# All three tiles of p transposed by DMA in batches 1 to 3, in an attention kernel that feeds two dense layers

## The chip, the cores and the metric

The kernel runs on one core of a Trainium2 chip. The metric is the time of one execution in microseconds, the median over the runs of one kernel. TensorE (PE in the profile), VectorE (DVE), ScalarE (ACT), GpSimd (POOL) and SyncE (SP, which here issues every DMA of the kernel) each work through their own list of instructions in order and wait for one another through semaphores.

## What is computed

```python
# q, k, v: (4 batches, 8 heads, 1152 rows, 64), float32
q_pool = q.reshape(B, H, S // 2, 2, D).mean(axis=3)          # 576 queries per head
scores = (1.0 / np.sqrt(D)) * np.matmul(q_pool, k.transpose(0, 1, 3, 2))
attn = np.exp(scores - np.max(scores, axis=-1, keepdims=True))
attn = attn / (np.sum(attn, axis=-1, keepdims=True) + 1e-09)
x = heads side by side of np.matmul(attn, v)                 # 2304 x 512
h = x @ w_in                                                 # 512 -> 2048
x = np.where(h >= 1, h, np.where(h <= -1, 0.0, (h + 1) ** 2 / 4)) @ w_out    # 2048 -> 512
out = np.maximum(np.maximum(x @ w1, x @ w2), x @ w3) @ w_out2                # 512 -> 768 -> 512
```

## The kernel before

Attention is cut into 48 **units**: batch (4), block of 192 queries (3 per batch), pair of heads (4). A unit's 2 x 192 queries fill three tiles of 128 rows: tile 0 has the even head's first 128 queries, tile 1 the odd head's first 128, tile 2 the remaining 64 of each head. For each tile, `soft` forms the scores against all 1152 keys on PE (three PSUM banks), DVE takes the row maximum, ACT the exponential into `pf`, with the row sums beside it. The product with v needs the tile transposed, keys on partitions, and `turned` does that. In batch 0 (`WHOLE`) all is float32 and PE transposes. In batches 1 to 3, 36 units, numbers go to PE as two float16 halves, "hi" (rounded) and "lo" (the rest):

- tiles 0 and 1: ACT writes hi and DVE writes lo into `hl`, and one DMA transpose, issued by SP, moves both halves into `pt`;
- tile 2: PE transposes the float32 tile in nine 128 x 128 pieces into PSUM (`tr`), ACT writes hi and DVE lo from there into `pt`.

`shares` adds the 1e-9 to the three row sums (POOL), takes reciprocals (DVE), spreads them (POOL), has PE turn them into one row per head, `rs`, and copies that to `R` (ACT). `av` multiplies `pt` with v on PE, and DVE multiplies the result by `R` and a scale into `xf`.

The first dense layer follows for each block of 192 queries: eight **up steps** (`up_step`, 24 products on PE each) and four **down steps** (`down_step`, 48 products each). They are the filler that stands between the attention units on every engine. The last four down steps are written out a second time by the generator `dense` behind the two tables (this stays so). The second dense layer comes last; its weights w1 to w3 are loaded and split by the steps `h` and `j`, its input by `Z`, all in the table `AFTER`.

The order on each engine is written out by hand: the tables `ATTENTION` and `AFTER` name one step after another (`s13.2` is a step of unit 13's tile 2, `r` of `shares`, `a` of `av`, `u` and `y` of an up or down step, `k`, `v`, `q` of loading and splitting), and each name records the next piece of that step's generator on whichever engines it uses. Nothing is reordered behind them.

`pf` has 2 buffers, `hl` 3 (the tile of k before its own DMA transpose takes one of these too), `pt` 2. Scores and `tr` share two places of three PSUM banks each. POOL also pools q and splits k, v and q; SP also issues the loads of q, k, v and weights, the transposes and copies of q and k, and the stores of the first layer's result y.

Of the kernel before, what the change touches and what calls it, by code (L numbers as in the profile page):

```python
# [7 lines left out]
F32 = mybir.dt.float32  # L8
F16 = mybir.dt.float16
# [3 lines left out]
ALU = mybir.AluOpType  # L13
# [135 lines left out]
def body(ctx: ExitStack, tc: tile.TileContext, q, k, v, w_in, w_out, w1, w2, w3, w_o2, out):  # L149
# [283 lines left out]
    def q_steps(b, i, p):  # L433
# [58 lines left out]
    def soft(b, i, p, who):  # L492
# [4 lines left out]
        if who == 0:  # L497
            sums[b, i, p] = small.tile([P, 3], F32, tag="sm", bufs=4, name=f"sm{b}_{i}_{p}")
# [683 lines left out]
```

## Time and profile before

| | |
|---|---|
| median of three runs | 1137.13 us (1136.02 to 1138.56) |
| the profiled execution | 1133.35 us |
| its span, first to last instruction | 1131.6 us |
| busy share of the span: PE, weight loads of PE, DVE, ACT, POOL | 93%, 77%, 77%, 68%, 20% |
| chain of work that ended last: PE, DVE, ACT, DMA | 53%, 3%, 2%, 2% of the span |
| granted TensorE clock over the execution | 0.988 |

Busy shares are means over stages of different kinds. Batch 0 of attention and the preparation of weights fill roughly the first 230 us, batches 1 to 3 with the first dense layer between them run to about 770 us, the rest of the first dense layer to 857 us, and the second dense layer to the end. A stage's own row tells which engine has no time left in it. A DMA share of 1.00 would be all 16 DMA engines busy; since packets overlap, single rows go above it.

### The profile page before, as it was taken

Reading aid. Unit: us, or ns where it says so; the run is one execution under the profiler, and the core shown is the slowest. Engines: PE = TensorE matmul, PEld = TensorE weight load, DVE = VectorE, ACT = ScalarE, POOL = GpSimd, SP = SyncE. Lnnn points to the kernel's source line nnn. Section 1 sums busy time; section 2 is a strip of 40 time slices with the busy share of each in tenths; the row PEclk is TensorE's granted clock in tenths of the full one; section 3 lists DMA queues with packets and bytes.
Section 4 is the critical chain, followed back from the end, with each engine's and each line's share of the span. In section 5 each row is a group of like instructions: output and inputs, shape, how many; then the busy total and the mean of one; then the engine's idle time right before and its main releaser. Section 6 shows DMA issues by size and latency. Waiting matters only on the chain.

```text
span 1131.6 us, 27049 instructions
## 1 busy us (share of the span) xinstructions
PE 1053.1 (93%) x11175; PEld 875.4 (77%) x11175; DVE 866.8 (77%) x1422; ACT 768.9 (68%) x1354; POOL 226.4 (20%) x305
## 2 busy tenths in 40 slices
PE   1578998899999989999999999999999999999998
PEld 1355875678888878888888888899998877767774
DVE  6998896788888889887998887877875868364441
ACT  6697797778788778887888887775774443353332
POOL 3333223422212242121223211100000106000000
PEclk9898998999999999999999999999999999999999
DMA  9964324478578887766897766455444100100001
GB/s 330 256 169 162 103 73 95 126 161 148 91 138 155 171 170 155 138 134 110 169 183 150 137 114 105 94 86 189 155 121 137 43 10 20 61 11 19 20 19 56
DMA packets 274443, 135.31 MB, mean 120 GB/s; under 512 B 229136, under 2 KB 257552, under 8 KB 273296
## 3 DMA queue, kind: packets, MB, share of 16 engines
q1 hardware_dynamic: 274320, 133.59, 52.2%
q8 instruction: 87, 1.43, 0.5%
q14 instruction: 36, 0.29, 0.1%
HBM read 62.39 MB, written 9.83 MB: 64 GB/s over the span
## 4 chain that ended last, share of the span: by engine, by line
PE 53%; DVE 3%; ACT 2%; DMA 2%; issue 1%; POOL 1%; POOLq 0%; ACTq 0%; DVEq 0%; SPq 0%
PE py L691 11%; PE p L922 9%; PE ph L663 8%; PE po L1085 6%; PE sc L488 4%; PE pa L1020 4%; PE av L596 4%; PE pb L1020 2%; PE tr L551 2%; DVE st L502 1%; PE pc L1020 1%; DMA pt<-hl 1%; ACT pf L509 1%; DMA vn<-in_v_dram 1%; DVE hl L575 0%
## 5 line engine op out<-in xcount | busy, mean ns | idle before, releaser
L502 DVE TENSOR_REDUCE st<-sc 128x1 f32<-128x1152 f32 x144 | 194.4, 1352 | 34.2 <-PE sc L488 33.8
L691 PE MATMUL py<-g,wou 128*128 128x192 f16 x2496 | 213.3, 246 | 1.8 <-ACT t L667 1.6
L691 PEld LDWEIGHTS <-wou 128*128 128x128 f16 x2496 | 207.2, 98 | 2.4 <-issue 2.0
L663 PE MATMUL ph<-xh,win 128*128 128x192 f16 x2304 | 205.3, 247 | 0.2
L663 PEld LDWEIGHTS <-win 128*128 128x128 f16 x2304 | 191.5, 99 | 8.6 <-issue 4.3
L509 ACT ACTIVATE pf<-sc,st,esc 128x1152 f32<-128x1152 f32 x144 | 188.6, 1310 | 13.7 <-DVE st L504 9.5
L488 PE MATMUL sc<-kst,qst 128*64 128x512 f16 (+3 forms) x1152 | 168.8, 333 | 20.8 <-DMA kst<-kpre 7.0
L488 PEld LDWEIGHTS <-qst 128*64 128x64 f16 (+1 forms) x1152 | 79.9, 106 | 83.6 <-issue 30.8
L922 PE MATMUL p<-yh,wm 128*128 128x288 f16 x864 | 107.1, 286 | 0.0
L551 PE MATMUL tr<-ident,pf 128*128 128x128 f32 x648 | 87.0, 284 | 19.2 <-ACT pf L509 19.0
L922 PEld LDWEIGHTS <-wm 128*128 128x128 f16 x864 | 84.5, 98 | 21.9
L575 DVE TENSOR_TENSOR hl<-pf,hl 128x1152 f16<-128x1152 f32 x72 | 98.4, 1366 | 3.8 <-ACT hl L573 3.7
L551 PEld LDWEIGHTS tr<-ident,pf 128*128 128x128 f32 x648 | 74.3, 147 | 26.2 <-ACT pf L509 19.4
L596 PE MATMUL av<-pt,vhl 128*64 128x192 f16 x1944 | 86.8, 247 | 1.6 <-DMA pt<-hl 1.6
L596 PEld LDWEIGHTS <-vhl 128*64 128x64 f16 x1944 | 79.7, 110 | 6.9 <-issue 3.3
L573 ACT ACTIVATE hl<-pf 128x1152 f16<-128x1152 f32 x72 | 83.6, 1161 | 1.3
L667 ACT ACTIVATE t<-ph,Uv 128x384 f32<-128x384 f32 x96 | 55.0, 574 | 35.5 <-PE ph L663 31.1
L1085 PE MATMUL po<-wo,h 128*128 128x512 f16 (+1 forms) x342 | 72.3, 368 | 0.0
L519 POOL TENSOR_SCALAR sm<-sm 128x3 f32<-128x3 f32 x48 | 21.2, 442 | 248.4 <-ACT pf L509 239.9
L675 ACT ACTIVATE g<-t,dgs 128x384 f16<-128x384 f32 x96 | 57.7, 609 | 6.4 <-DVE t L673 5.6
L561 DVE TENSOR_TENSOR pt<-tr,pt 128x1152 f16<-128x1152 f32 x36 | 48.7, 1354 | 16.6 <-ACT pt L559 16.3
L677 DVE SCALAR_TENSOR_TENSOR g<-t,dgs,g 128x384 f16<-128x384 f32 x96 | 59.7, 632 | 2.1 <-ACT g L675 1.8
(211 smaller groups left out, 1565.4 us busy)
## 6 DMA issues: line engine op xcount, KB each, us to landing
vn<-in_v_dram SPq DMA_DIRECT2D x16, 576.0 KB, 4.7
kn<-in_k_dram SPq DMA_DIRECT2D x16, 576.0 KB, 4.8
raw_m<-in_moe_w_dram SPq DMA_DIRECT2D x12, 768.0 KB, 4.7
raw_in<-in_moe_w_in_dram SPq DMA_DIRECT2D x8, 1024.0 KB, 7.0
qn<-in_q_dram SPq DMA_DIRECT2D x24, 256.0 KB, 3.1
raw_ou<-in_moe_w_out_dram SPq DMA_DIRECT2D x10, 512.0 KB, 4.4
y_d<-ys SPq DMA_DIRECT2D x52, 96.0 KB, 2.1
qst<-qst SPq DMA_DIRECT2D x48, 96.0 KB, 2.3
```

What stands on the lines that cost most here:

```text
L488: nc.tensor.matmul(sc[m0:m1, n0:n1], qst[b, i, p][who][:, var, m0:m1], ks[:, h, n0:n1], start=(var == 0), stop=(var == 1))
L502: nc.vector.tensor_reduce(out=m, in_=sc, axis=AX.X, op=ALU.max, negate=True)
L509: nc.scalar.activation(out=pf, in_=sc, func=AF.Exp, bias=nb, scale=e, accum_out=sums[b, i, p][:, who:who + 1])
L551: nc.tensor.transpose(tr[:, c * P:(c + 1) * P], pf[:, c * P:(c + 1) * P], ident)
L573: nc.scalar.activation(out=hl[:, 0], in_=pf, func=AF.Copy)
L575: nc.vector.tensor_tensor(out=hl[:, 1], in0=pf, in1=hl[:, 0], op=ALU.subtract)
L596: nc.tensor.matmul(acc[64 * h:64 * h + 64], vhl[b, p][:, vi, h, c, :], pt[:, h, pi * KT + c, :], start=(c == 0 and e == 0), stop=(c == KT ...
L663: nc.tensor.matmul(ph[:, a], win[:, wi, kt, ff * P:(ff + 1) * P], x[:, xi, kt], start=(kt == 0 and e == 0), stop=(kt == KD - 1 and e == 2))
L691: nc.tensor.matmul(py, wou[:, ff // 2, wi, ff % 2, m * P:(m + 1) * P], g[:, gi, ff, :], start=(ff == 0 and e == 0), stop=(ff == NF - 1 and ...
L922: nc.tensor.matmul(ph[:, :NB2], wm[:, wi, i, kt, ff * P:(ff + 1) * P], yh[:, yi, kt, n0:n0 + NB2], start=(kt == 0 and e == 0), stop=(kt == ...
L1020: nc.tensor.matmul(ps[:, :NB2], w(wi, kt), x[:, xi, kt], start=(first and kt == 0 and e == 0), stop=(kt == 1 and e == 2), skip_group_check ...
L1085: nc.tensor.matmul(po, hh[:, hi, ff, t * P:(t + 1) * P], wo[:, wi, ff, c0:c1], start=(n == 0 and e == 0), stop=(n == NF2 - 1 and e == 2))
```

## The change

In batches 1 to 3, `turned` now does the same for all three tiles: POOL adds to the tile's own column of row sums and DVE takes its reciprocal; ACT writes hi and DVE lo from `pf`, both multiplied by that share; one DMA transpose moves both into `pt`. PE no longer transposes these tiles, `shares` is not called there, and `xf` needs only the scale, so ACT reads the product out of PSUM. `pt` is laid out as one row of 384 columns: tile 0, tile 2, tile 1. For that the odd head's queries are taken in another order, its first 64 rows into tile 2 and the following 128 into tile 1, so a q load that was one DMA for four head parts is now two. The small tiles `esc`, `sm` and `rb` have more buffers. In batch 0 only the spreading of tile 2's reciprocals is done in another way. Both tables are written anew.

```diff
-OWN_BANK = (True, False)
+BY_DMA = lambda b, i, p: True
+FOLD = False
 ATTENTION = """
-s42.0 s42.2 u8.6 u8.5 s42.1 u8.6 a41 s42.2 s42.1 s43.0 a41 s42.2 s42.1 u8.7 u8.6 s43.0 r42 s42.1 s42.2 u8.7 r42
+s41.2 s42.0 u8.7 s41.2 s41.1 s42.1 s41.2 s42.0 u8.6 s42.2 u8.5 s42.0 u8.6 y7.3 s41.2 s42.0 s42.2 s41.2 s42.1
...
     def q_steps(b, i, p):
-        load_q.dma_start(out=qn[:, 0:4].rearrange("p a r d -> p a (r d)"),
-                         in_=q[b, h0:h0 + 4, r0:r1].rearrange("h (p r) d -> p h (r d)", r=2))
+        shift = 0 if WHOLE(b, p) else P
+        for h in range(2 if shift else 1):
+            hs, r = (slice(h0 + h, h0 + 4, 2), r0 + h * shift) if shift else (slice(h0, h0 + 4), r0)
+            load_q.dma_start(out=qn[:, h:4:2 if shift else 1].rearrange("p a r d -> p a (r d)"),
+                             in_=q[b, hs, r:r + 2 * P].rearrange("h (p r) d -> p h (r d)", r=2))
...
     def turned(b, i, p, who, pf):
-            if not WHOLE(b, p):
-                tr = tr.rearrange("p (c h q) -> p h c q", c=KT, h=2)
-                hi, lo = pt[:, :, 0:KT, P:NB], pt[:, :, KT:2 * KT, P:NB]
-                nc.scalar.activation(out=hi, in_=tr, func=AF.Copy)
-                nc.vector.tensor_tensor(out=lo, in0=tr, in1=hi, op=ALU.subtract)
...
+        share = sums[b, i, p][:, who:who + 1]
+        at_ = slice(*((0, P), (2 * P, 3 * P), (P, 2 * P))[who])
+        nc.gpsimd.tensor_scalar(out=share, in0=share, scalar1=1e-9 * 2.0 ** 12, scalar2=2.0 ** -15, op0=ALU.add,
+                                op1=ALU.mult)
+        nc.vector.reciprocal(out=share, in_=share)
...
         hl = hlp.tile([P, 2, KT * P], F16, tag="hl", name=f"hl{key}")
-        nc.scalar.activation(out=hl[:, 0], in_=pf, func=AF.Copy)
-        nc.vector.tensor_tensor(out=hl[:, 1], in0=pf, in1=hl[:, 0], op=ALU.subtract)
-        nc.sync.dma_start_transpose(out=pt[:, who, :, 0:P], in_=hl.rearrange("p a b -> p (a b)"))
+        nc.scalar.activation(out=hl[:, 0], in_=pf, func=AF.Copy, scale=share)
+        nc.vector.scalar_tensor_tensor(out=hl[:, 1], in0=pf, scalar=share, in1=hl[:, 0], op0=ALU.mult, op1=ALU.subtract)
+        nc.sync.dma_start_transpose(out=new_pt(b, i, p)[:, :, at_], in_=hl.rearrange("p a b -> p (a b)"))
...
     def av(b, i, p):
-        nc.vector.scalar_tensor_tensor(out=xf[b, i][:, p, :], in0=acc, scalar=Uv[b][:, p:p + 1], in1=R.pop((b, i, p)),
-                                       op0=ALU.mult, op1=ALU.mult)
+            nc.scalar.activation(out=xf[b, i][:, p, :], in_=acc, func=AF.Copy, scale=Uv[b][:, p:p + 1])
```

How the tables move instructions is seen in the recorded order of each engine. First PE in batch 3, block 1, around tile 2 of pair 1 (names end in block, pair, tile and a buffer number; `tr` is the transposed tile, `py` and `ph` are down and up steps). Before:

```order
L551 MATMUL tr_1_1_2_10194<-ident,pf_1_1_2_10147 128x128 x9
L691 LDWEIGHTS wou
L691 MATMUL py_1_2_10207<-g_1_8505,wou 128x192
...
L488 LDWEIGHTS qst_1_2_9630
L488 MATMUL sc_1_2_1_10270<-kst_2_8727,qst_1_2_9630 128x512
...
L528 MATMUL tr_1_1_2_10194<-ident,rb_1_1_10191 128x128
L529 MATMUL tr_1_1_2_10194<-rb_1_1_10191,halves 128x64
L663 LDWEIGHTS win
L663 MATMUL ph_2_6_10285<-xh_2_8936,win 128x192
```

The changed kernel at the same place, from tile 2 of pair 1 to the product with v of pair 0:

```order
L498 MATMUL sc_1_1_2_9848<-kst_1_7971,qst_1_0_8775 64x512
...
L498 LDWEIGHTS qst_1_2_9367
L498 MATMUL sc_1_2_0_9865<-kst_2_8538,qst_1_2_9367 128x512
...
L696 LDWEIGHTS win
L696 MATMUL ph_2_6_9882<-xh_2_8778,win 128x192
...
L630 LDWEIGHTS vhl_0_7914
L630 MATMUL av_1_0_9916<-pt_1_0_9626,vhl_0_7914 64x192
```

The nine transposes of tile 2 and the two instructions that turn the sums are gone from PE, and the product with v of pair 0 now stands behind the scores of pair 1's last tile and pair 2's first. Over the whole of PE's list, 14 up steps and 15 down steps stood behind the last product with v; now 12 and 14 do, so two up steps and one down step have moved ahead of it.

DVE at the same place (`st` is the row maximum, `hl` lo of a tile, `sm` a reciprocal, `g` a piece of an up step). Before:

```order
L610 SCALAR_TENSOR_TENSOR xf_1_10104<-av_1_0_10028,Uv_9055,R_1_0_10083 128x192
L677 SCALAR_TENSOR_TENSOR g_2_9500<-t_2_2_3_9949,dgs_6817,g_2_9500 128x384
L502 TENSOR_REDUCE st_1_1_2_10118<-sc_1_1_2_10091 128x1
L575 TENSOR_TENSOR hl_1_1_1_10108<-pf_1_1_1_10089,hl_1_1_1_10108 128x1152
L502 TENSOR_REDUCE st_1_2_0_10177<-sc_1_2_0_10111 128x1
...
L561 TENSOR_TENSOR pt_1_1_10106<-tr_1_1_2_10194,pt_1_1_10106 128x2x9x64
```

And now, for the three tiles of pair 1:

```order
L581 RECIPROCAL sm_1_1_9722<-sm_1_1_9722 128x1
L512 TENSOR_REDUCE st_1_1_2_9875<-sc_1_1_2_9848 128x1
L600 SCALAR_TENSOR_TENSOR hl_1_1_0_9861<-pf_1_1_0_9783,sm_1_1_9722,hl_1_1_0_9861 128x1152
L512 TENSOR_REDUCE st_1_2_0_9912<-sc_1_2_0_9865 128x1
L600 SCALAR_TENSOR_TENSOR hl_1_1_1_9908<-pf_1_1_1_9844,sm_1_1_9722,hl_1_1_1_9908 128x1152
...
L581 RECIPROCAL sm_1_1_9722<-sm_1_1_9722 128x1
L512 TENSOR_REDUCE st_1_2_1_10025<-sc_1_2_1_9979 128x1
...
L581 RECIPROCAL sm_1_2_9911<-sm_1_2_9911 128x1
L600 SCALAR_TENSOR_TENSOR hl_1_1_2_10027<-pf_1_1_2_9972,sm_1_1_9722,hl_1_1_2_10027 128x1152
```

Lo of tile 2 is formed from `pf` like the others, one reciprocal stands ahead of each lo, and the multiplication into `xf` is no longer here.

SP in batch 2, block 1, pairs 1 and 2 (`pt` from `hl` is the transpose of a tile, `qst` and `qn` belong to q, `y_d` is a store of y). Before:

```order
L578 DMA_TRANSPOSE pt_1_1_6903<-hl_1_1_0_6826 128x18x128
L460 DMA_TRANSPOSE qst_2_0_6952<-qpre_2_0_6342 128x6x128
L578 DMA_TRANSPOSE pt_1_1_6903<-hl_1_1_1_6925 128x18x128
L463 DMA qst_2_0_6952<-qst_2_0_6952 64x768 x2
L440 DMA qn_0_2_7083<-in_q_dram 128x4x128
L443 DMA qn_0_2_7083<-in_q_dram 64x2x128 x2
L578 DMA_TRANSPOSE pt_1_2_7103<-hl_1_2_0_7080 128x18x128
L698 DMA y_d_67<-ys_1_2_7098 128x192
L578 DMA_TRANSPOSE pt_1_2_7103<-hl_1_2_1_7184 128x18x128
```

Now:

```order
L602 DMA_TRANSPOSE pt_1_1_6841<-hl_1_1_0_6765 128x18x128
L473 DMA qst_2_0_6763<-qst_2_0_6763 64x768 x2
L602 DMA_TRANSPOSE pt_1_1_6841<-hl_1_1_1_6779 128x18x128
L602 DMA_TRANSPOSE pt_1_1_6841<-hl_1_1_2_6922 128x18x128
L602 DMA_TRANSPOSE pt_1_2_7023<-hl_1_2_0_6945 128x18x128
L731 DMA y_d_67<-ys_1_2_6974 128x192
L449 DMA qn_1_0_7087<-in_q_dram 128x2x128 x2
L453 DMA qn_1_0_7087<-in_q_dram 64x2x128 x2
L602 DMA_TRANSPOSE pt_1_2_7023<-hl_1_2_1_7084 128x18x128
```

Each unit has three transposes where it had two, a q load is two issues of 128 partitions and two of 64 where it was one and two, and a store or a load stands behind one transpose more.

## Rows read from the trace of the kernel before

**Rows 1.** Windows of two stages: length, busy us (instructions) of each engine, clock, DMA.

```profile
230.00:770.10 540.10, 527.00 (x6674) 465.13 (x6671) 461.77 (x677) 429.95 (x776) 123.16 (x198) 1.00 0.72 136
770.10:857.40 87.30, 87.30 (x1059) 87.28 (x1058) 65.67 (x111) 55.95 (x98) 0.90 (x1) 1.00 0.47 156
```

**Rows 2.** Timeline of PE near 690 us: start, length, engine, line, out<-in, count.

```profile
690.45 1.15 PE L551 MATMUL tr<-ident,pf 128*128 128x128 f32 x9
...
691.44 4.12 PE L691 MATMUL py<-g,wou 128*128 128x192 f16 x48
695.40 1.14 PE L488 MATMUL sc<-kst,qst 128*128 128x512 f16 x6
696.37 0.28 PE L528 MATMUL tr<-ident,rb 128*128 128x128 f32 x1
...
696.75 0.93 PE L596 MATMUL av<-pt,vhl 128*64 128x192 f16 x18
```

**Rows 3.** Groups by line: count, busy us, mean ns, idle before and its releasers.

```profile
L575 DVE TENSOR_TENSOR hl<-pf,hl 128x1152 f16<-128x1152 f32 x72 | 98.4, 1366 | 3.8 <-ACT hl L573 3.7
...
L596 PE MATMUL av<-pt,vhl 128*64 128x192 f16 x1944 | 86.8, 247 | 1.6 <-DMA pt<-hl 1.6
...
L573 ACT ACTIVATE hl<-pf 128x1152 f16<-128x1152 f32 x72 | 83.6, 1161 | 1.3
...
L561 DVE TENSOR_TENSOR pt<-tr,pt 128x1152 f16<-128x1152 f32 x36 | 48.7, 1354 | 16.6 <-ACT pt L559 16.3
...
L559 ACT ACTIVATE pt<-tr 128x1152 f16<-128x1152 f32 x36 | 40.4, 1123 | 5.1 <-PE tr L551 4.9
...
L695 ACT ACTIVATE ys<-py,yd 128x192 f32<-128x192 f32 x52 | 21.6, 415 | 28.8 <-PE py L691 23.8 <-DMA y_d<-ys 3.1 <-issue 1.4
L610 DVE SCALAR_TENSOR_TENSOR xf<-av,Uv,R 128x192 f32<-128x192 f32 x48 | 20.0, 416 | 16.9 <-PE av L596 12.7 <-PE av L591 1.3 <-ACT st L507 0.8
L532 ACT ACTIVATE R<-tr 128x192 f32<-128x192 f32 x36 | 11.9, 329 | 4.9 <-PE tr L529 4.7
L521 DVE RECIPROCAL sm<-sm 128x3 f32<-128x3 f32 x48 | 8.1, 169 | 5.2 <-POOL sm L519 4.1
```

**Rows 4.** Instructions on the split v: ns shortest, median, longest; first and last start.

```profile
L374 DVE SCALAR_TENSOR_TENSOR vhl<-vn,sb,vhl x12: 1382/1414/2381, 201.1 to 618.2; 128x1152 f16<-128x1152 f32 x12
```

**Rows 5.** Windows of 40 us with DVE above 36 us, same columns as rows 1.

```profile
240.00:280.00 40.00, 38.76 (x503) 33.93 (x502) 36.26 (x53) 30.99 (x59) 8.04 (x13) 1.00 0.87 167
400.00:440.00 40.00, 34.95 (x433) 31.29 (x432) 37.33 (x53) 31.63 (x58) 17.01 (x16) 1.00 0.85 173
560.00:600.00 40.00, 38.74 (x489) 33.71 (x489) 36.85 (x56) 33.69 (x62) 10.28 (x14) 1.00 0.97 191
600.00:640.00 40.00, 39.52 (x496) 35.03 (x492) 37.57 (x57) 32.69 (x62) 14.66 (x19) 1.00 0.69 129
```

**Rows 6.** Instructions on pt: the transposes' issue on SP's queue, and their landing.

```profile
L578 SPq DMA_TRANSPOSE pt<-hl x72: 2456/2728/4997, 224.1 to 761.1; - x72
...
DMA to landing us min/median/max: 4.5/4.9/8.0
```

**Rows 7.** Windows around one transpose that runs alone, issued at 718.33 us.

```profile
718.00:724.00 6.00, 6.00 (x73) 5.99 (x71) 4.35 (x8) 4.53 (x9) 1.24 (x4) 1.00 0.53 98
720.00:722.00 2.00, 2.00 (x25) 1.99 (x24) 1.50 (x4) 1.97 (x5) 0.00 (x0) 1.00 1.17 216
```

**Rows 8.** Instructions on qn: the issue of a q load.

```profile
L443 SPq DMA_DIRECT2D qn<-in_q_dram x48: 595/644/2142, 3.5 to 640.7; - x48
```

**Rows 9.** Instructions on qst: the transpose of a q tile.

```profile
L460 SPq DMA_TRANSPOSE qst<-qpre x24: 1211/1244/2115, 18.7 to 700.2; - x24
```

**Rows 10.** Instructions on kpre: the transpose of a tile of k.

```profile
L412 SPq DMA_TRANSPOSE kst<-kpre x16: 2473/2802/6019, 25.7 to 602.5; - x16
```

**Rows 11.** Timeline of DVE: the last pieces of the second layer's first input.

```profile
845.07 2.28 DVE L867 SCALAR_TENSOR_TENSOR yh<-yf,ysc,yh 128x576 f16<-128x576 f32 x3 [0.56 <-ACT yh L865]
```

**Rows 12.** Chain that ended last, at the second layer's first products: start, us, count.

```profile
857.45 26.46 PE p L922 x216
```

More of the change, by code (lines that the diff above doesn't have):

```diff
@@ L469, in exp_scale @@
     def exp_scale(b, i, p):
-        e = small.tile([P, 1], F32, tag="esc", bufs=3, name=f"esc{b}_{i}_{p}")
+        e = small.tile([P, 1], F32, tag="esc", bufs=8, name=f"esc{b}_{i}_{p}")
         nc.gpsimd.tensor_scalar(out=e, in0=ub[b][:, p, 0:1], scalar1=esc[b, i, p], scalar2=0.5 / float(D) ** 0.5,
@@ L497, in soft @@
         if who == 0:
-            sums[b, i, p] = small.tile([P, 3], F32, tag="sm", bufs=4, name=f"sm{b}_{i}_{p}")
+            sums[b, i, p] = small.tile([P, 3], F32, tag="sm", bufs=6, name=f"sm{b}_{i}_{p}")
         e = esc[b, i, p]
@@ L539, in new_pt @@
         if (b, i, p) not in PT:
-            PT[b, i, p] = ptp.tile([P, 2, 2 * KT, NB], F16, tag="pt", name=f"pt_{b}_{i}_{p}")
+            shape = [P, 2, 2 * KT, NB] if WHOLE(b, p) else [P, 2 * KT, 2 * NB]
+            PT[b, i, p] = ptp.tile(shape, F16, tag="pt", name=f"pt_{b}_{i}_{p}")
         return PT[b, i, p]
@@ L544, in turned @@
         key = f"{b}_{i}_{p}_{who}"
-        if who == 2 or WHOLE(b, p):
-            tr = place(f"tr{key}")
-            rs = tr[:, KT * P:KT * P + NB]
-            tr = tr[:, :KT * P]
+        if WHOLE(b, p):
+            tr = place(f"tr{key}")[:, :KT * P]
             for c in range(KT):
@@ L552, in turned @@
             yield
-            if who == 2 and not OWN_BANK[b > 0]:
-                R[b, i, p] = rs
-            pt = new_pt(b, i, p)
-            if not WHOLE(b, p):
-                tr = tr.rearrange("p (c h q) -> p h c q", c=KT, h=2)
-                hi, lo = pt[:, :, 0:KT, P:NB], pt[:, :, KT:2 * KT, P:NB]
-                nc.scalar.activation(out=hi, in_=tr, func=AF.Copy)
-                yield
-                nc.vector.tensor_tensor(out=lo, in0=tr, in1=hi, op=ALU.subtract)
-                yield
-                return
-            pt = whole(pt)
+            pt = whole(new_pt(b, i, p))
             if who < 2:
@@ L595, in av @@
                 for h in HO:
-                    nc.tensor.matmul(acc[64 * h:64 * h + 64], vhl[b, p][:, vi, h, c, :], pt[:, h, pi * KT + c, :],
+                    nc.tensor.matmul(acc[64 * h:64 * h + 64], vhl[b, p][:, vi, h, c, :],
+                                     pt[:, pi * KT + c, h * NB:h * NB + NB],
                                      start=(c == 0 and e == 0), stop=(c == KT - 1 and e == 2))
+        if i == 0 and not WHOLE(b, p):
+            weigh(b, p)
         yield
```

276 lines of the change are left out of this document (155 added, 121 removed).

## Prediction

> **What bounds the kernel now.** I read the windows by stage first. From 230 to 770 us, where batches 1 to 3 run, PE is busy for 527.0 of 540.1 us at a clock of 1.00; DVE is busy for 461.8 (85%), ACT for 430.0 (80%), POOL for 123, and the DMA share is 0.72 [rows 1]. PE has 13.1 us without work in the whole stage, so the stage is as long as PE's list. Behind it, up to 857.4 us, PE is busy without a gap [rows 1]. The groups by line agree: the product with v has waited for a transpose for only 1.6 us in 1944 instructions [rows 3]. What leaves PE's list in this stage should come off the time, as long as the other engines keep up. That condition is the question, because they are not far from full.
>
> **What PE loses.** The nine transposes of a tile start at 690.45 and the next product starts at 691.44: 0.99 us. The instructions on the sums start at 696.37 and the next product at 696.75: 0.38 us [rows 2]. There are 36 such units: 36 x (0.99 + 0.38) = 49.3 us. Nothing is put in their place on PE. In batch 0 the replacement of one small instruction by another is costed at nothing, since batch 0 lies in a stage where PE has time to spare.
>
> **What the other engines get.** On DVE, lo of 108 tiles is now a product and a difference in one instruction. Today 72 of them take 1.366 us and 36 take 1.354 us [rows 3]. The nearest row for the new form has the same shape, inputs and instruction, the split of v: 1.382 shortest, 1.414 median, 2.381 longest [rows 4]. I take the median, as it is the same instruction: 108 x 1.414 = 152.7 against 72 x 1.366 + 36 x 1.354 = 147.1, so +5.6 us; the bounds are nothing, at today's duration, and the longest row for a part of them (a rival, below). Reciprocals become 108 instead of 36, at 0.169 each: +12.2. The multiplication into xf leaves: 36 x 0.416 = 15.0 [rows 3]. The sum is +2.8 us. With two up steps more in the stage (some 1.5 us of DVE each, estimated from today's load) DVE needs 461.8 + 2.8 + 3 = 468 us.
>
> On ACT, hi of tile 2 takes 1.161 instead of 1.123, R leaves (0.329), and xf comes; a copy of the same shape out of PSUM with a scale takes 0.415 [rows 3]. That is 36 x (0.038 - 0.329 + 0.415) = +4.5 us, on an engine that is 80% busy: hidden. POOL gets two small additions more per unit and loses two spreads, at a load of 123 of 540 us: hidden too, as long as an addition does not stand behind a long split there.
>
> **Transposes.** 36 more of them go through SP's queue and the DMA engines. One is issued in 2.73 us (2.46 to 5.00) and lands 4.9 us after its issue began (4.5 to 8.0) [rows 6]. One that runs alone takes a DMA share of 0.53 over 6 us, 3.2 us of all engines; while it runs the share is 1.17, which I take as full rate [rows 7]. The mean share of the stage becomes (0.72 x 540.1 + 36 x 3.2) / 519 = 0.97, with 519 us the new length found below: 83% of full rate. A rule of the Trainium skill speaks against all this: VectorE: DVE Perf Modes, section "The three transpose paths", gives the DMA path 1309 ns for a 128 x 128 block and TensorE 390 ns. By that page a tile's 18 blocks (nine of hi, nine of lo) would take, as an estimate, 23.6 us by DMA, one behind another, and 36 tiles more would make the kernel hundreds of microseconds longer. The row has all 18 landed in 4.9 us, so the trace does not agree, and by the trace the term is the 3.2 us of DMA above.
>
> Does a transpose come in time? From hi of tile 2 to the landing it is 1.16 + 1.41 + 4.9 = 7.5 us, with a small addition and a reciprocal ahead. A unit takes 519 / 36 = 14.4 us, and the product with v stands behind the next unit's last and the following unit's first scores, so there is cover of about one unit. A buffer of hl is held for the same 7.5 us, 10.6 if the landing takes 8.0; three buffers serve 108 tiles and 12 tiles of k in 519 us, 13.0 us for each. It fits, without much to spare.
>
> **How long the stage becomes.** Two up steps and one down step come in from behind, 2 x 24 + 48 = 96 products. The down step's 48 take from 691.44 to 695.40 us, 3.96 us, until the next starts [rows 2], and an up step's products have the same shape, so this is 7.9 us, and PE's list is 527.0 - 49.3 + 7.9 = 485.6 us. Its gaps grow, as DVE fills up. In the four windows in which DVE is busy for more than 36 of 40 us, PE lacks 1.24, 5.05, 1.26 and 0.48 us, 2.0 in the mean [rows 5]. At that share the stage takes 485.6 / 0.95 = 511 us, with 25.6 us of gaps instead of 13.1: 12.5 us given back. DVE then works 468 of 511 us, 92%, as in those windows. Further, loads of k, v and q are not spread evenly. The window 560 to 600 us has a DMA share of 0.97 already [rows 5], 38.8 us; with 2.7 units of the third transpose (8.6 us) it needs 47.4 / 1.17 = 40.5 us, and only 38.4 are there. Over by 2 us in such a window, and the new tables may bunch the loads more: for all loads of the stage I take 8 us together, between nothing and about 20 (2 us in each of ten windows of the stage). So 511 + 8 = 519 us.
>
> The stage behind it loses 7.9 us of PE's work. There the second layer's input is ready at 847.35 us [rows 11] while its first product starts at 857.45 [rows 12]; of these 10.1 us 2.2 remain. It costs nothing if the weights' steps start as long ahead as now; if they start late, at most the 7.9.
>
> The sum: -49.3 + 12.5 + 8 = -28.8 us. From the profiled execution, 1133.35 us (1.75 us outside its span of 1131.6), that gives 1104.6; the median stands 3.8 above that execution, so I forecast 1108 us.
>
> **Rivals.** (1) *Nothing is given back.* PE's gaps stay as they are; for it speaks that the scores no longer share their PSUM places with a fourth tile per unit; against it, rows 5. The time is 1137.1 - 49.3 = 1088 us.
>
> (2) *DVE becomes the bound.* If one lo in four takes the longest row's 2.38 instead of 1.41 [rows 4], that is 27 x 0.97 = 26 us more, 494 in all. At 37.0 of 40 us, the mean of the four windows in which DVE is fullest [rows 5], this needs 534 us; with the 7.9 us taken from behind, the kernel is 14 us shorter: 1123 us. For it speaks the longest row, against it that the median lies close to the shortest.
>
> (3) *SP's queue becomes the bound, and the kernel slower.* For a batch of 12 units its issues are 36 x 2.73 = 98.3, four of k at 2.80 [rows 10], six of q at 1.24 [rows 9], and 24 q loads, 12 copies and 20 other loads and stores, none taken above a q load's 0.64 [rows 8]: 98.3 + 11.2 + 7.4 + 35.8 = 153 us, of 173 available, 88%; now it is 116 of 180. SP waits in order for data too, so it does not reach 100%. If the DMA engines back up and an issue takes 3.87 us, halfway to the longest, a batch takes 139 + 54 = 194 us even without a wait, the stage 581, and the time is 1137 + 41 - 8 = 1170 us. It decides from a mean issue of 3.56 us on, where a batch takes (540.1 + 7.9) / 3 = 183 us. The Trainium skill, Perfetto Trace Analysis, section "What 'DMA-bound' means", names this bound: an issuing track solid with DMA slices is descriptor generation, not data movement. The trace agrees so far that over half of a transpose's 4.9 us is its issue.
>
> (4) *No difference.* Only if gains and these costs cancel; no row says that PE's work was hidden.
>
> **How the numbers follow.** My forecast with its own range, 1098 to 1118 (the DMA term between nothing and 20): 0.57. Rival 1, to below 1098: 0.14. Rival 2, 1118 to 1134: 0.13. Within 0.2%, which is about what a measurement of this kernel can tell from no change: 0.05. Rival 3: 0.11. So faster 0.84, same 0.05, slower 0.11. The range from 1088 to 1138 leaves out rival 3, and a few in 100 below rival 1.
>
> **What would show it.** Right: PE without L551 in the stage, the stage near 519 us, its gaps near 33 us and ended by DVE or by `pt`, the DMA share near 0.97, lo near 1.41. Rival 3: issues of a transpose above 3.5 us, and the product with v or ACT's hi waiting for DMA. Rival 2: lo well above 1.41, or scores waiting for DVE. I would be wrong if the stage's gaps exceed 60 us, or if the first 230 us, whose steps are in a new order too, change by more than a few.

## The result: 1.3% faster, and the profile after

The changed kernel takes 1119.38 us (median of 4 runs, 1116.86 to 1121.73) against 1136.58 of the kernel before; the ratio is 0.9868, with a 95% interval of 0.9834 to 0.9901. Measured again beside the first experiments it was 0.9894 (0.9872 to 0.9916). The forecast was 1108 us. The direction held, and so did the wide range of 1088 to 1138 us; the forecast's own narrower range, 1098 to 1118 us, was just missed. Of the 28.8 us of gain that it expected only 12 to 15 came by these ratios.

The windows of the profiled execution (1121.73 us, span 1119.7), cut where the changed kernel's stages end; columns as in [rows 1]:

```profile
0.00:230.00 230.00, 177.09 (x1579) 135.28 (x1580) 203.31 (x350) 195.17 (x297) 67.34 (x94) 0.96 0.64 175
230.00:765.80 535.80, 496.07 (x6223) 427.48 (x6222) 444.55 (x696) 427.03 (x761) 108.72 (x183) 0.98 0.94 173
765.80:845.10 79.30, 79.30 (x962) 79.30 (x963) 62.49 (x104) 53.47 (x92) 0.91 (x1) 1.00 0.51 170
845.10:1119.70 274.60, 269.58 (x1972) 192.52 (x1970) 151.37 (x309) 102.56 (x216) 28.12 (x15) 1.00 0.11 37
```

Against [rows 1], the stretch behind the last product with v fell from 87.3 to 79.3 us, and the second layer after it kept its length. So the two up steps and the down step that moved ahead left that stretch in full. But the stage of batches 1 to 3, which by the forecast's figures lost some 41 us of PE's work (49.3 less 7.9), ends only 4.3 us earlier. PE has 39.7 us without work there (535.80 less 496.07) where it had 13.1, its clock is 0.98 instead of 1.00, and the DMA share is 0.94 instead of 0.72. DVE is busy for 83%: it is not the bound.

Who ended PE's waits in that stage (us in total, times, longest):

```profile
PE av L630 <- DMA pt<-hl: 11.3, 6, 4.7
PE ph L696 <- ACT py L729: 7.8, 4, 4.6
PE sc L498 <- ACT pf L519: 5.2, 9, 1.2
PE py L724 <- ACT t L700: 5.0, 2, 4.4
```

No large one is ended by DVE. The first is a landing; the others are ACT, and the groups by line show what ACT and DVE wait for in turn:

```profile
L600 DVE SCALAR_TENSOR_TENSOR hl<-pf,sm,hl 128x1152 f16<-128x1152 f32 x108 | 152.5, 1417 | 13.6 <-ACT hl L598 13.3
L598 ACT ACTIVATE hl<-pf,sm 128x1152 f16<-128x1152 f32 x108 | 134.1, 1247 | 32.3 <-issue 13.8 <-DMA pt<-hl 13.8 <-DVE sm L581 2.7
L630 PE MATMUL av<-pt,vhl 128*64 128x192 f16 x1944 | 91.8, 254 | 15.5 <-DMA pt<-hl 11.3 <-ACT t L700 2.9 <-ACT ys L728 1.1
...
L581 DVE RECIPROCAL sm<-sm 128x1 f32<-128x1 f32 x108 | 16.9, 157 | 20.5 <-POOL sm L578 19.2
L644 ACT ACTIVATE xf<-av,Uv 128x192 f32<-128x192 f32 x36 | 14.9, 413 | 12.3 <-PE av L630 12.0 <-issue 0.2
```

Lo (1.417 us) and xf (0.413) cost what the forecast said. Hi does not: 1.247 us with the share as its factor, where [rows 3] have 1.161 without one; that is 9 us of ACT over 108 tiles. ACT's hi waited for 1.3 us in all before the change, and waits for 32.3 now. The product with v, which waited 1.6 us for landings [rows 3], waits 11.3.

The transposes, with the rows that answer to [rows 6]:

```profile
L602 SPq DMA_TRANSPOSE pt<-hl x108: 2457/2859/5033, 217.3 to 756.9; - x108
...
DMA to landing us min/median/max: 4.5/5.2/8.0
```

One is a little dearer than before, 2.86 us against 2.73 to issue and 5.2 against 4.9 to land (medians). What grew more is the time ahead of the issue: from the end of lo to the issue of its transpose over the 108 tiles in the trace, the median is 1.29 us, with one in ten above 4.0; before, over 72 tiles, it was 0.06 and 1.2.

The clock, around the largest gap, which the landing of `pt` ends at 381.1 us; three windows:

```profile
376.00:379.00 3.00, 0.38 (x2) 0.30 (x2) 2.83 (x5) 2.50 (x3) 0.00 (x0) 1.00 1.13 243
379.00:385.80 6.80, 4.66 (x55) 4.41 (x56) 5.48 (x9) 4.33 (x9) 2.09 (x2) 0.50 1.05 195
385.80:390.00 4.20, 4.20 (x46) 3.73 (x47) 3.81 (x9) 3.64 (x6) 3.05 (x3) 1.00 1.02 244
```

PE has had almost no work since 376.4 us; its clock falls to the lower level, 1.2 GHz, while it still waits, and is back at 2.4 GHz 6.8 us later, after 4.66 us of work at half speed. There are six such stretches after 232 us (one more lies across the cut at 230); their sum, with PE's work in them:

```profile
sum 23.80, PE 21.47 PEld 19.50 DVE 19.75 ACT 18.01 POOL 6.77; mean PE 3.58 PEld 3.25 DVE 3.29 ACT 3.00 POOL 1.13
```

The same 21.47 us of work would take half as long at 2.4 GHz, so up to 10.7 us are lost. Each stands at one of the stage's six longest gaps, 2.6 to 4.7 us. Before the change the longest gap of the stage was 1.57 us, and no stretch of it ran at half clock.

### The profile page after: what moved, and what is told of

It reads as the page before. It is cut to its first block, busy times and chain, and to the rows that moved or that the text cites. A ratio compares the mean times of both kernels' runs of the same rounds, so it can differ in the third digit from the quotient of the medians.

```text
span 1119.7 us, 26302 instructions
## 1 busy us (share of the span) xinstructions
PE 1022.0 (91%) x10731; PEld 834.6 (75%) x10731; DVE 861.7 (77%) x1458; ACT 778.2 (70%) x1366; POOL 205.1 (18%) x293
## 4 chain that ended last, share of the span: by engine, by line
PE 55%; DMA 7%; DVE 6%; issue 5%; ACT 3%; SPq 1%; POOL 1%; ACTq 0%; POOLq 0%; DVEq 0%
PE py L724 13%; PE p L955 9%; PE ph L696 8%; PE po L1118 6%; PE av L630 5%; PE sc L498 5%; PE pa L1053 4%; DMA pt<-hl 4%; PE pb L1053 2%; DVE hl L600 2%; DMA qn<-in_q_dram 1%; DVE st L512 1%; ACT hl L598 1%; PE pc L1053 1%; DMA kn<-in_k_dram 1%
## 5 line engine op out<-in xcount | busy, mean ns | idle before, releaser
L724 PE MATMUL py<-g,wou 128*128 128x192 f16 x2496 | 216.6, 248 | 5.7 <-ACT t L700 5.0
L600 DVE SCALAR_TENSOR_TENSOR hl<-pf,sm,hl 128x1152 f16<-128x1152 f32 x108 | 152.5, 1417 | 13.6 <-ACT hl L598 13.3
L598 ACT ACTIVATE hl<-pf,sm 128x1152 f16<-128x1152 f32 x108 | 134.1, 1247 | 32.3 <-issue 13.8
L630 PE MATMUL av<-pt,vhl 128*64 128x192 f16 x1944 | 91.8, 254 | 15.5 <-DMA pt<-hl 11.3
L630 PEld LDWEIGHTS <-vhl 128*64 128x64 f16 x1944 | 84.3, 114 | 22.1 <-issue 16.7
L578 POOL TENSOR_SCALAR sm<-sm 128x1 f32<-128x1 f32 x108 | 34.3, 318 | 286.7 <-ACT pf L519 282.1
L1118 PEld LDWEIGHTS <-h 128*128 128x128 f16 x342 | 33.5, 98 | 34.1
L706 DVE SCALAR_TENSOR_TENSOR t<-t 128x384 f32<-128x384 f32 x96 | 56.3, 586 | 3.3
L566 PE MATMUL tr<-ident,pf 128*128 128x128 f32 x324 | 43.8, 286 | 10.3 <-ACT pf L519 9.9
```

Source lines behind the costliest of these rows:

```text
L598: nc.scalar.activation(out=hl[:, 0], in_=pf, func=AF.Copy, scale=share)
L600: nc.vector.scalar_tensor_tensor(out=hl[:, 1], in0=pf, scalar=share, in1=hl[:, 0], op0=ALU.mult, op1=ALU.subtract)
L630: nc.tensor.matmul(acc[64 * h:64 * h + 64], vhl[b, p][:, vi, h, c, :], pt[:, pi * KT + c, h * NB:h * NB + NB], start=(c == 0 and e == 0), ...
L724: nc.tensor.matmul(py, wou[:, ff // 2, wi, ff % 2, m * P:(m + 1) * P], g[:, gi, ff, :], start=(ff == 0 and e == 0), stop=(ff == NF - 1 and ...
L1118: nc.tensor.matmul(po, hh[:, hi, ff, t * P:(t + 1) * P], wo[:, wi, ff, c0:c1], start=(n == 0 and e == 0), stop=(n == NF2 - 1 and e == 2))
```

## Experiments

Theory 1: the added transposes fill SP's list and the DMA engines, so p, q and k come late, PE gets gaps, and the clock takes something on top of each. Theory 1a puts it on SP's list, 1b on the DMA engines. Theory 2: ACT is late, because hi became dearer (theory 3, the clock alone, has no run of its own). Theory 4: three buffers for `hl` are too few. Each run's time stands as its ratio to the kernel before, with the 95% interval; us are differences of these ratios to the changed kernel's 0.9894, times 1134 us, and are good to some 3.5 us. The changed kernel itself stands beside hl4, half_turn and hi_plain; the other runs have only the kernel before beside them. Gaps, clock and share are those of the windows from 230 us to the last product with v.

| run | median us | ratio | to the changed kernel | stage us | PE gaps us | PE clock | DMA share |
|---|---|---|---|---|---|---|---|
| after_again | 1121.79 | 0.9894 (0.9872 to 0.9916) | | 536.9 | 37.0 | 0.97 | 0.94 |
| hl4 | 1118.96 | 0.9870 (0.9847 to 0.9892) | -2.7 | 531.4 | 38.5 | 0.98 | 0.95 |
| half_turn | 1089.79 | 0.9620 (0.9598 to 0.9642) | -31.1 | 505.4 | 16.9 | 0.99 | 0.66 |
| hi_plain | 1116.09 | 0.9847 (0.9825 to 0.9868) | -5.3 | 530.0 | 35.1 | 0.98 | 0.95 |
| two_turns | 1143.00 | 1.0091 (1.0072 to 1.0110) | +22.3 | 560.2 | 54.8 | 0.96 | 0.92 |
| plain_pool | 1181.84 | 1.0409 (1.0374 to 1.0444) | +58.4 | 598.9 | 72.0 | 0.96 | 0.94 |
| more_bytes | 1137.97 | 1.0053 (1.0034 to 1.0072) | +18.0 | 551.6 | 52.8 | 0.97 | 0.98 |
| best | 1132.67 | 0.9996 (0.9978 to 1.0014) | +11.6 | 552.1 | 49.9 | 0.97 | 0.93 |
| before_36 | 1161.53 | 1.0232 (1.0208 to 1.0255) | | 568.8 | 33.5 | 0.98 | 0.92 |
| third_half | 1106.93 | 0.9759 (0.9737 to 0.9781) | -15.3 | 522.2 | 28.7 | 0.98 | 0.86 |
| two_turns_late | 1113.35 | 0.9820 (0.9797 to 0.9843) | -8.4 | 526.9 | 31.1 | 0.98 | 0.99 |
| once4 | 1111.18 | 0.9797 (0.9777 to 0.9817) | -11.0 | 531.0 | 38.7 | 0.98 | 0.95 |

**after_again**: no edit.

> The changed kernel once more, beside the next three. Every theory expects 0.983 to 0.990 of the kernel before, some 1117 to 1122 us, with about 40 us of gaps on PE from 230 us to the end of the last product with v and several stretches there at half the TensorE clock.

As expected; the six runs lie between 1119.32 and 1123.41 us.

**before_36**, the cost alone, in the kernel before:

```diff
         nc.sync.dma_start_transpose(out=pt[:, who, :, 0:P], in_=hl.rearrange("p a b -> p (a b)"))
+        if who == 1:
+            nc.sync.dma_start_transpose(out=spare, in_=hl.rearrange("p a b -> p (a b)"))
```

> The kernel before, with the cost of the change alone: in batches 1 to 3 tile 1 is turned a second time into a tile that nothing reads, 36 transposes more on SP's queue and the DMA engines, as many as the change adds. PE, DVE and ACT have the same instructions as in the kernel before, PE's own transposes among them. Theory 1 (the transposes' load on SP's list and the DMA engines gives the gain back): the share of the stage rises from 0.72 to above 0.9 and PE's gaps from 13 us to 30 us or more, with stretches at half clock: 15 to 35 us slower than before, a ratio of 1.013 to 1.031. Rival 5 (it is the order of the new tables that makes the gaps, not the load): under 5 us slower.

26.3 us slower (0.0232 x 1134.6). The window of its stage, and PE's longest waits in it:

```profile
230.00:798.80 568.80, 535.30 (x6652) 472.03 (x6651) 459.02 (x671) 426.63 (x770) 114.06 (x198) 0.98 0.92 166
```

```profile
PE sum_k L193 <- ACT kpre L390: 6.8, 2, 3.8
PE sum_v L193 <- ACT vhl L390: 6.5, 3, 3.6
PE sc L489 <- ACT pf L510: 5.4, 5, 1.7
PE av L599 <- DMA pt<-hl: 3.7, 4, 2.3
```

Nothing reads the 36 added transposes, the tables are the old ones, and yet PE's gaps grow by 20.4 us and the clock falls as in the changed kernel. Here it is mostly the loads of k and v that come late, not p: ACT, which ends PE's two longest waits, has itself waited 9.0 us for k and 10.9 us for v. So 36 more transposes alone can cost this much, and rival 5, the new order, is not needed for it. One difference is left: the added transposes follow directly on tile 1's own and hold its `hl` longer (ACT's hi waits 3.4 us for that), so they do not stand in time where the change has them.

**half_turn**:

```diff
-        nc.sync.dma_start_transpose(out=new_pt(b, i, p)[:, :, at_], in_=hl.rearrange("p a b -> p (a b)"))
+        nc.sync.dma_start_transpose(out=new_pt(b, i, p)[:, KT:2 * KT, at_], in_=hl[:, 1])
-                                     pt[:, pi * KT + c, h * NB:h * NB + NB],
+                                     pt[:, KT + c, h * NB:h * NB + NB],
```

> Left out: the transpose of hi. Only lo is turned, nine blocks instead of 18, after the same waits, and the product with v reads lo in both places, so that PE, ACT and DVE have the same instructions as in the changed kernel, and SP has as many issues, each of half the bytes. Theory 1: an issue in the stage falls from 3.06 to about 1.6 us, the DMA share from 0.94 to about 0.7, PE's gaps in the stage from 40 to 13 to 20 us and most half-clock stretches go: 25 to 37 us shorter, 1083 to 1095 us. Theory 2 (ACT): within 4 us of the changed kernel. Theory 4 (buffers): in part, 5 to 12 us, as a buffer is held for some 2.5 us less.

31.1 us shorter, with the same instructions on PE, ACT and DVE. The stage, and the transposes:

```profile
230.00:735.40 505.40, 488.50 (x6227) 420.40 (x6227) 451.42 (x701) 425.76 (x764) 120.02 (x185) 0.99 0.66 121
```

```profile
L602 SPq DMA_TRANSPOSE pt<-hl x108: 1242/1311/3870, 219.8 to 724.8; - x108
...
DMA to landing us min/median/max: 3.2/3.4/7.2
```

An issue takes half as long for half the blocks, DVE is busier than in the changed kernel (451.42 of 505.4 us, 89%) and still PE has 22.8 us less without work than in the profiled execution above. That rules out DVE's and ACT's own work as the main bound of the changed kernel. It halves SP's work and the engines' alike, so it does not part 1a from 1b.

**third_half**, the same in every third unit:

```diff
+        half = (4 * i + p) % 3 == 2
-        nc.sync.dma_start_transpose(out=new_pt(b, i, p)[:, :, at_], in_=hl.rearrange("p a b -> p (a b)"))
+        nc.sync.dma_start_transpose(out=new_pt(b, i, p)[:, KT:2 * KT, at_] if half else new_pt(b, i, p)[:, :, at_],
+                                    in_=hl[:, 1] if half else hl.rearrange("p a b -> p (a b)"))
```

> Left out: the transpose of hi in every third unit of batches 1 to 3 (12 of 36, nine blocks instead of 18 for their three tiles), whose product with v reads lo in both places. It takes 36 half transposes from SP and the DMA engines, a third of what the run with all of them took, which was 32 us shorter than the changed kernel. If each transpose costs the same (the cost goes with SP's and the engines' work): 9 to 13 us shorter, a ratio of 0.978 to 0.982. If it costs only above some load (the engines full): 16 us or more shorter, 0.975 or less. Theory 2 (ACT): within 3 us.

15.3 us shorter, between the two expectations, near the second: a third of the relief brings about half of the gain. With an error of 3.5 us this is just clear of a third (10.4 us).

**more_bytes**:

```diff
+        if who == 2:
+            nc.gpsimd.dma_start(out=spare[12 * b + 4 * i + p], in_=words(w1[:P, :256]))
```

> Added: a copy of 256 KB from DRAM to DRAM per unit of batches 1 to 3, 36 in all, issued by POOL, whose result is not used. At the 333 GB/s that the first slice of the page shows at a share of 0.99 that is 0.8 us of all DMA engines each, 28 us in the stage, whose share of 0.94 has no room for it. SP's list is unchanged. Theory 1b (the DMA engines): transposes land later, 10 to 28 us slower than the changed kernel. Theory 1a (SP's list): under 5 us slower.

18.0 us slower. PE's wait for landings of `pt` grows from 11.3 to 17.3 us and that of its scores for ACT from 5.2 to 8.7:

```profile
PE av L633 <- DMA pt<-hl: 17.3, 9, 5.4
PE sc L499 <- ACT pf L520: 8.7, 12, 1.6
```

SP's list got no instruction more, so load on the DMA engines costs time without it. How much of the 18.0 us is theirs alone is not shown: POOL's list got 36 issues of 0.58 us, and hi's wait for the reciprocal behind POOL's additions grew from 2.7 to 6.9 us. The Trainium skill, Perfetto Trace Analysis, section "What 'DMA-bound' means", names the DMA engines and the issuing sequencer as two of the things that a DMA-bound kernel can be bound on; in this run the engines are the one that was loaded, while SP's issues also took longer (3.26 us in the mean against 3.06).

With 3.2 us of DMA time for one transpose [rows 7], three runs suggest a curve. Taking away 58 us of DMA time in third_half brought 15.3 us (0.27 for each us), the other 115 in half_turn 15.8 (0.14), and adding 28 cost 18.0 (0.64). By these estimates a DMA is dearer the fuller the stage is. The last of them hangs on the 0.8 us of a copy, which is an estimate too; by the windows' shares (0.98 x 551.6 less 0.94 x 536.9) the copies took some 36 us, which makes it 0.50. And two_turns_late, below, does not lie on the curve: its share is 0.99 against the changed kernel's 0.94, and it is faster.

**two_turns** and **two_turns_late**. The first issues hi's nine blocks directly behind hi, the second both halves where the one issue stood:

```diff
         nc.scalar.activation(out=hl[:, 0], in_=pf, func=AF.Copy, scale=share)
+        nc.sync.dma_start_transpose(out=new_pt(b, i, p)[:, 0:KT, at_], in_=hl[:, 0])   # two_turns
...
-        nc.sync.dma_start_transpose(out=new_pt(b, i, p)[:, :, at_], in_=hl.rearrange("p a b -> p (a b)"))
+        nc.sync.dma_start_transpose(out=new_pt(b, i, p)[:, 0:KT, at_], in_=hl[:, 0])   # two_turns_late
+        nc.sync.dma_start_transpose(out=new_pt(b, i, p)[:, KT:2 * KT, at_], in_=hl[:, 1])
```

> The transpose of a tile as two issues of nine blocks: hi right behind ACT's hi, lo behind DVE's lo. The same blocks and bytes. In the run with nine blocks an issue took 1.43 us against 3.06 for 18, so SP has as much to do as before. Theory 1a (SP's list: what is late is the issue, with 1.7 us in the mean between the end of lo and the issue of its transpose): hi's half goes out 1.4 us and more earlier, in time that SP now waits, the last half lands some 3.75 us after its issue instead of 5.39, PE's gaps fall from 37 to 40 us to 20 to 28 and the kernel gets 10 to 18 us shorter, a ratio of 0.972 to 0.980 to the kernel before. Theory 1b (the DMA engines are full): within 5 us of the changed kernel, 0.984 to 0.992.

22.3 us slower: a miss for both theories. SP's timeline in that run shows one place where it happens:

```profile
587.61 0.57 SPq L732 DMA_DIRECT2D y_d<-ys  x1
590.81 1.88 SPq L599 DMA_TRANSPOSE pt<-hl  x1
592.74 0.57 SPq L389 DMA_DIRECT2D vn<-in_v_dram  x1
```

SP stands still from 588.2 to 590.8 us until ACT's hi is there, and the load of v behind it in the list, which waits for nothing of the kind, goes out late; ACT waits for such loads next, longer than in the changed kernel, where the same three waits are 5.5, 1.8 and 0.6 us:

```profile
ACT qpre L462 <- DMA qst<-qpre: 13.6, 7, 3.4
ACT vhl L395 <- DMA vn<-in_v_dram: 12.5, 4, 4.3
...
ACT hl L598 <- DMA kst<-kpre: 8.0, 5, 2.7
```

> The transpose of a tile as two issues of nine blocks, both where the one of 18 stands now, behind lo. It asks why the run with hi's half behind hi was 21 us slower than the changed kernel. If it was SP's wait for hi, with the loads behind it in SP's list: within 4 us of the changed kernel, 0.985 to 0.993. If twice as many transposes cost that: 15 us or more slower, 1.003 or above.

8.4 us shorter than the changed kernel, more than the 4 us expected. So twice as many issues cost nothing, and what cost two_turns its time is the place of hi's issue in SP's list: 30.7 us lie between the two, with the same blocks, bytes and issues. That the wait which stands at that place does it, with the loads behind it, is read from the rows above and from no run of its own. That splitting gains by itself was not expected; the share rises to 0.99, but no run tells why.

**plain_pool**:

```diff
-    load_q, copy_q = nc.sync, nc.sync
+    load_q, copy_q = nc.gpsimd, nc.gpsimd
```

> All plain loads, copies and stores of the first part are issued by POOL instead of SP; the transposes stay on SP; the bytes are the same. From 230 us to the last product with v they are some 79 of the 446 us that SP spends on issues. Theory 1a (SP's list): the wait from lo to its issue falls from 1.7 us to under 0.8, PE's gaps to 20 to 28 us, 8 to 18 us shorter than the changed kernel. Theory 1b (the DMA engines): landings still take 5.4 us, within 5 us of the changed kernel. What could hide 1a: POOL does its splits between the issues, so a load can come late there; then q or k loads show up in PE's waits.

58.4 us slower; it does not decide between 1a and 1b, because POOL's list holds the loads far longer than SP's did:

```profile
POOL sm L578 <- ACT pf L519: 207.5, 68, 9.6
POOL qn L457 <- DMA qn<-in_q_dram: 50.6, 13, 6.7
```

POOL waits for exp, then for its own q loads, and everything behind is late. The wait from lo to its issue did fall, to 0.91 us in the mean from 1.69, though not under 0.8. But the transposes, now almost alone on SP, land no sooner, with a median of 6.0 us instead of 5.2:

```profile
DMA to landing us min/median/max: 4.5/6.0/23.9
```

The Trainium skill, DMA: Bandwidth & Descriptors, section "Issuing engines are not separate DMA queues", says that the engines are shared whoever issues; this run, with its 6.0 us, agrees.

**hl4**:

```diff
-    hlp = at.enter_context(tc.tile_pool(name="hlp", bufs=3, side="right"))
+    hlp = at.enter_context(tc.tile_pool(name="hlp", bufs=4, side="right"))
```

> A fourth buffer for hl, nothing else. Theory 1 (the transposes come late because SP's list and the DMA engines are nearly full): the issues stand in the same order behind the same loads, so within 5 us of the changed kernel. Theory 4 (three buffers are too few: hi waits until a transpose has landed): the 13.8 us that ACT's hi waits for landings fall under 4, and the kernel gets 8 to 15 us shorter, 1104 to 1111 us. Theories 2 (ACT is late because hi became dearer) and 3 (only the clock) expect no change of more than 3 us.

2.7 us shorter, not told from nothing. The wait that theory 4 named did go:

```profile
L598 ACT ACTIVATE hl<-pf,sm 128x1152 f16<-128x1152 f32 x108 | 133.9, 1246 | 19.2 <-issue 15.4 <-DVE sm L581 2.9 <-DMA pt<-hl 0.7
```

From 13.8 us to 0.7, and PE's gaps stayed at 38.5. Where ACT's gain went is only partly seen: it waits longer elsewhere (9.0 us instead of 5.5 for transposes of q, for one), and from lo to its issue it is still 1.72 us in the mean, against 1.69. Theory 4, 8 to 15 us for the buffer, falls.

**hi_plain**:

```diff
-        nc.scalar.activation(out=hl[:, 0], in_=pf, func=AF.Copy, scale=share)
+        nc.scalar.activation(out=hl[:, 0], in_=pf, func=AF.Copy)
```

> Left out: the division in hi, which ACT writes from pf without the factor share; lo still multiplies by share. Theory 2: hi falls from 1.247 to about 1.161 us, ACT gets 9 us less to do in 108 tiles and the kernel 5 to 12 us shorter. Theory 1: within 4 us of the changed kernel, since what is late is behind hi and lo; hi also no longer waits for the reciprocal, which is worth less than 3 us by its waits in the trace.

5.3 us shorter, at the lower end of theory 2 and, with its error, not clear of theory 1's 4 us:

```profile
L598 ACT ACTIVATE hl<-pf 128x1152 f16<-128x1152 f32 x108 | 124.1, 1154 | 16.1 <-DMA pt<-hl 14.9 <-DMA kst<-kpre 1.1
```

Hi costs 1.154 us again, and with the factor its 13.8 us of "issue" went too. In the trace of the changed kernel these are four waits, and each ends 0.08 us after a reciprocal. The longest of them, with what stands ahead of it on POOL and DVE:

```profile
618.97 1.00 POOL L457 TENSOR_TENSOR qn<-qn 128x384 f32<-128x384 f32 x1 [7.92 <-DMA qn<-in_q_dram]
621.14 0.19 POOL L578 TENSOR_SCALAR sm<-sm 128x1 f32<-128x1 f32 x1
622.55 0.16 DVE L581 RECIPROCAL sm<-sm 128x1 f32<-128x1 f32 x1
622.79 1.25 ACT L598 ACTIVATE hl<-pf,sm 128x1152 f16<-128x1152 f32 x1 [5.23 <-issue]
624.57 1.76 PE L724 MATMUL py<-g,wou 128*128 128x192 f16 x11 [4.37 <-ACT t L700]
```

POOL waits for a load of q, pools it and splits v; only then comes the addition that hi has depended on since the change, and PE's third longest gap stands at the end of the chain. In three of the four waits it is a q load that POOL had waited for. In hi_plain the gap at this place is not among the long ones. So late DMAs reach PE by this path too. The price of hi and this wait were not parted, and theory 2 holds at most as a small addition.

**best** and **once4**. In both kernels the last four down steps are computed twice, since the last loop does not look whether a step has run. Both runs leave the second time out and have four buffers for `hl`; best also has the two issues of two_turns.

```diff
         for job in down:
-            run(down_step(*job))
-            yield
-            yield
+            if ("y", *job) not in begun:
+                run(down_step(*job))
+                yield
+                yield
```

> Candidate for a faster version: two issues per transpose, a fourth buffer for hl, and the last four down steps, which both kernels compute twice, computed once. The third part takes 15.9 us from PE, of which the chain that makes the second layer's input leaves about 6.9 us (its last piece is ready at 838.2 us where the first product starts at 845.1). Theory 1a: 10 to 18 us for the issues and up to 3 for the buffer, so 1095 to 1105 us, a ratio of 0.965 to 0.975. Theory 1b: 7 to 10 us in all, 0.979 to 0.983.

> Candidate for a faster version: the changed kernel with a fourth buffer for hl, and the last four down steps, which both kernels compute twice, computed once. 1 to 3 us for the buffer and about 6.9 us for the steps: 8 to 10 us shorter than the changed kernel, a ratio of 0.979 to 0.983. If the second layer's input comes later than in the changed kernel, only the buffer's part.

best misses, as it contains two_turns' issues: it is 10.7 us faster than two_turns, about what once4 (11.0 us) gains on the changed kernel. once4 comes out as expected and is the fastest version run that computes everything: 1111.18 us, 0.9797 (0.9777 to 0.9817) of the kernel before. Of the 15.9 us of PE's work that it saves, 8.3 us appear (against hl4); the first products of the second layer then wait for their input, 6.2 us. Whether it adds up with two_turns_late is not shown.

## Why the prediction held, and where it put the gain too high

**What PE loses** was right: the 36 units' transposes and the instructions on the sums are gone. **The seam** was right: 79.3 us where 87.3 less 7.9 was forecast, at no cost.

**The stage** came out at 535.8 us instead of 519, and 16.8 us is the whole miss of the profiled execution (span 1119.7 against 1104.6 less 1.75). It has two parts. The gaps are 39.7 us, where 519 less 485.6, 33.4, was forecast: 6.3 more. And 10.7 us at half clock were in no term of the sum. PE's work without the half clock is 496.07 less 10.7, 485.3 us, and agrees with the forecast's 485.6 only because two things cancel (other terms, below).

**The step that failed** is the reason for the gaps. They were worked out as 12.5 us from a full DVE and 8 us for all transposes and loads. DVE was 83% busy and released no large wait of PE, and in half_turn it was 89% busy with only 16.9 us of gaps. The term of the DMAs is the one mis-sized: 36 such transposes alone cost 26.3 us in before_36, gaps and clock together, not 8, between nothing and 20. The forecast took the cost as the DMA time that does not fit into a window at full rate; before_36 shows that it begins below that, at a mean share of 0.92. The rows show how it reaches PE: in the changed kernel a transpose is issued 1.29 us behind lo instead of 0.06, loads come late as well, and PE waits for the latest of them. How much of it is SP's list in order and how much the shared engines, theories 1a and 1b, no run parts.

That the time still came out within 12 us is in part luck: the 12.5 us that were put on DVE did not come, and the transposes cost some 18 us more than their 8. The measured 1119.38 us lies in the interval that was given to rival 2, whose mechanism did not happen.

**"It fits, without much to spare"** was near the mark: `hl` was held for 10.5 us in the mean, the longest landing's 10.6 rather than 7.5, and the cover of one unit for the product with v was used up in six places, up to 4.7 us.

**Rival 3**, SP's queue, showed one of its two signs: the product with v and ACT's hi do wait for DMAs, 11.3 and 13.8 us, but the mean issue was 3.06 us in the stage, under its 3.56 (2.94 before; the forecast's 2.73 is the median), and SP was busy for 446 of 535.8 us, 83%. What it names took at most a part of the gain. **Rival 2** did not happen: lo stayed at 1.417. **Rival 1** is what half_turn comes close to, 1089.8 us against 1088.

**Other terms.** ACT's hi was taken at 1.161 us and costs 1.247; hi_plain puts 5.3 us on it and its wait. POOL was taken as hidden "as long as an addition does not stand behind a long split there"; it stood behind the pooling of a late q, as the rows under hi_plain show. The first 230 us did change by more than a few, which the forecast had named as a sign of being wrong. PE is busy there for 177.09 us against 169.31, as one up step, one down step and some scores now run in them; DVE has 15.3 us more to do there, and so less in the stage than the forecast's 468. The row before:

```profile
0.00:230.00 230.00, 169.31 (x1479) 130.63 (x1481) 187.99 (x326) 180.47 (x265) 74.24 (x91) 0.94 0.60 165
```

Since that work is no longer behind 230 us, the stage's remaining list must have become some 7 us dearer than the forecast's prices to come out at 485.3. It is not the product with v: its 91.8 us against 86.8 hold 10.03 us of work at half clock, half of which is already taken off above. Read from the trace with the half clock taken off, they are spread over all products of the stage, some 1 to 2% on each; why stays open.

If these costs add up, 49.3 us gained on PE less 26.3 for the transposes' load and 5.3 for hi leave 17.7; 12 to 15 were measured. What remains, 3 to 6 us, is about the size of the errors of these differences, and stays open.

## What to carry to other kernels

Work moved from a full engine to the DMA engines was paid for here before they were full: 26.3 us for going from a share of 0.72 to 0.92. To price such a move, add the same transfers to the old kernel with nothing reading them, as before_36 does, and read the gaps of the bound engine. Before adding a wait to a queue that issues in order, read what stands behind it: the same transfers cost 30.7 us more with one more wait for each tile, though half of each was allowed to start earlier. A large wait that a buffer removes (13.8 us here) can be worth next to nothing (2.7 us, not clear of noise) when other things in line are late as well. And a new input, as hi's share here, ties an engine to everything that stands ahead of that input's maker.

## What the hardware showed that was not expected

A gap of PE cost more than its length here: six gaps of 2.6 to 4.7 us were each followed or ended by 3.4 or 6.8 us at 1.2 GHz, up to 10.7 us in all, in a stage that had run at 2.4 GHz throughout before the change. An ACT copy of 128x1152 with a factor from a tile takes 1.247 us, without one 1.154. An issue of a DMA transpose takes 1.31 us for nine blocks and 2.86 for 18 (medians), and two_turns_late, with two issues of nine, is not slower than the changed kernel. Below nine it does not go on falling like that: the six blocks of a q tile take 1.24 us [rows 9].
